# A gated FFT-mixer and token-MLP kernel: front, D-pass columns, inverse order and stores rearranged

## The chip, the cores and the metric

The kernel runs on one core of a Trainium2 chip (trn2). The metric is the device time of one execution in microseconds (us). The engines are TensorE (PE, with its weight loads PEld), VectorE (DVE), ScalarE (ACT), GpSimd (POOL) and SyncE (SP), whose queue issues most of the transfers. ACT and POOL can issue transfers too.

## The reference, cut to what matters

```python
def _A_ref(x, w_r, w_i):                # x: (1, 2048, 512) bf16
    X = rfft2(x.astype(float32))        # over tokens and channels
    return irfft2(X * (w_r + 1j * w_i), s=(2048, 512)).astype(bfloat16)

def _B_ref(x, w1, b1, w2, b2):          # w1: (2048, 1792), w2: (1792, 2048)
    h = _layernorm(x)                   # over the 512 channels, eps 1e-5
    u = gelu_tanh(einsum("bsd,sf->bdf", h, w1) + b1)
    return (einsum("bdf,fs->bds", u, w2) + b2).transpose(0, 2, 1)

x = A_x
g = sigmoid((x * gate_w).sum(-1, keepdims=True))
out = g * _A_ref(x, A_w_r, A_w_i) + (1 - g) * _B_ref(x, B_w1, B_b1, B_w2, B_b2)
```

All inputs are bf16. The tokens are cut into 16 blocks of 128.

## The kernel before, in words

Two computations share PE. The token MLP is the large one; the Fourier filter is cut into small matrix products between DVE butterflies.

**Front.** SP issues the loads of x (`load_x`, L90) and of the first 1024 columns of w1 (`load_w1a`, L93) in turn, in growing pieces; x blocks 4 and 5 come in one load. The two bias vectors go as rows into `brow` by two loads on ACT's queue (L120, L121). PE multiplies a zero tile, `warm`, ten times (L238), turns the biases into columns with one product against an identity (L240, `pb`), and starts the first MLP product (`mm1`, L271): for each of the first 12 blocks its 8 feature tiles, then, tile by tile in the order 0, 2, 4, 6, 1, 3, 5, 7, the last four blocks, each tile followed by its gelu on ACT (L336). The u tiles 0 to 5 lie in three PSUM pairs of two banks; tiles 0 and 1 share a pair.

**Layer norm.** For blocks 0 to 5 DVE does the statistics (`bstat`, L245), the aggregate (L249) and an addition of eps (L251), POOL raises to the power -0.5 (L254), and DVE normalises (`norm_dve`, L267). Blocks 6 to 15 go in pairs: aggregate on DVE, small operations on POOL (L251, L253, L254, L258), normalisation on ACT (`norm`, L263). Beside this ACT makes the sine tables: TD from DVE's angles (`angles_d`, `sines_d`), the angles for TA (L292, L293), TA (`sines_a`).

**Filling.** From the end of `mm1` (L271) on the program's order on PE is written by a small planner at build time. `products()` yields the remaining 128x512 products one by one: w1's other 6 tiles (L430), then w2's 15 blocks of 14 products (L439), each block ended by ACT's scale and bias (L442, `tbv`) and, late, by `final`. `fill(n)` takes n of them, `fill_to(t)` takes them until the planner's clock, which begins at 33.2 and gains 0.2165 a product, has reached t; `spent` adds the time of Fourier products. The constants T_TA, T_TB, T_IA, T_IB and T_Y say at which clock the token pass of YA, that of YB, the two inverses and the output scaling are put in.

**Fourier part.** DVE folds x into YA and YB (L365 to L419). For each of four residues r, `token` (L482, L485, L486) multiplies with the token tables into a PSUM pair, which ACT copies to ZA or ZB (L487); `dpass` (L494) multiplies with the channel tables TD into a pair, whose copy (L496) interleaves the two halves t of each column. DVE then splits, applies the filter and sums (`split`, `weights`, `sums`). `inverse` runs per residue `inv_tok` (L611, L617) and `inv_d` (L632), each emptied by ACT (`evac`, L589). There are three PSUM pairs in all, used in turn; a product into a pair waits until its last content is copied. DVE adds the residues up (L658 to L697), ACT and DVE scale with the gate, and DVE forms the filter's output `ap_` (L718 to L727).

**Gate.** DVE multiplies x with gate_w (`gprod`), ACT sums each block (`gacc`, L282, 16 blocks), then a tanh (L549) and three POOL operations give omg, gs and ombb2. ACT's w2 blocks need omg and ombb2.

**End.** `final(b)` adds ap_ to tbv on DVE (L730) and stores on SP (L731). The last block is done in two halves of 256 columns (L749), each ended by one DVE operation (L751) and its store (L753); ACT adds the bias to its part of ap_ before (L744). `hook` calls `final` for the blocks that the planner emits after T_Y + 12; those done by then are added in one loop.

Of the kernel before, what the change touches and what calls it, by code (L numbers as in the profile page):

```python
# [11 lines left out]
BF16 = mybir.dt.bfloat16  # L12
# [11 lines left out]
T_TA, T_TB, T_IA, T_IB, T_Y = 45.3, 56.8, 71.0, 83.8, 102.4  # L24
# [19 lines left out]
def kernel(  # L44
# [47 lines left out]
    def load_w1a(b0, b1):  # L92
        nc.sync.dma_start(out=w1a[b0 // 4][:, b0 % 4:(b1 - 1) % 4 + 1], in_=w1v[:, b0:b1, 0:FT1 * P])  # L93
# [24 lines left out]
    load_x(0, 1)  # L118
    brow = small.tile([NFT + NB, P], BF16, name="brow")
    nc.scalar.dma_start(out=brow[0:NFT], in_=B_b1.rearrange("(ft f) -> ft f", f=P))  # L120
    nc.scalar.dma_start(out=brow[NFT:NFT + NB], in_=B_b2.rearrange("(b a) -> b a", a=P))  # L121
    for b in range(3):
        load_x(b + 1, b + 2)
        load_w1a(b, b + 1)
# [16 lines left out]
    consts = small.tile([P, 5], F32, name="consts")  # L141
# [4 lines left out]
    nc.vector.memset(consts[:, 4:5], 1536.0)  # L146
    c_mpi, c_pi, c_mhalf = consts[:, 0:1], consts[:, 1:2], consts[:, 2:3]
# [86 lines left out]
    warm = small.tile([P, D], BF16, name="warm")  # L234
    nc.vector.memset(warm[:], 0.0)  # L235
# [188 lines left out]

    def products():
# [63 lines left out]
    def dpass(r, Z, cs):  # L489
        pr = pair("dp")  # L490
        for q, (sc, lst, t) in enumerate(((0, 0, 1), (1, 1, 0), (1, 2, 0), (0, 2, 1))):
            for c in range(2):
                o = 2 * c + q // 2
                nc.tensor.matmul(pr[:, sc, o * P:(o + 1) * P], lhsT=Z[:, r, q, c], rhs=TD[:, lst, t],  # L494
                                 start=True, stop=True)
        nc.scalar.copy(cs[:, :, r].rearrange("p x (j t) -> p x t j", t=2),  # L496
                       pr[:].rearrange("p h (c t j) -> p (h c) t j", c=2, t=2))
# [45 lines left out]
    for r in range(4):  # L543
# [3 lines left out]
    gacc(12, 16)  # L547
# [9 lines left out]
    fill_to(T_TB)  # L557
    ZB = H(6, [P, 4, 4, 2, P], "ZB")
    for r in range(4):
        token(1, r, ZB, YB)  # L560
        spent(0.87)
        fill(2)
# [25 lines left out]
    def evac(out, pr):  # L588
        nc.scalar.copy(out, pr[:].rearrange("p h n -> p (h n)"))  # L589
        act[0] = max(act[0], clock[0] + 0.1) + 1.01  # L590
# [31 lines left out]
    def inv_d(g, r, R, Hh):  # L622
        room()
# [10 lines left out]
        spent(0.44)  # L634
        evac(Hh[:, r].rearrange("p c n -> p (c n)"), pr)

    def inverse(g, UV, gslot, hslot, order):
# [97 lines left out]
    def hook(b):  # L735
        final(b)
# [44 lines left out]
```

## Time and profile before

| What | us |
|---|---|
| median of 3 runs (lowest, highest) | 130.16 (129.43, 131.82) |
| the profiled execution's own time | 130.46 |
| its span, from first to last instruction | 128.0 |
| ten zero products, first start to last end | 1.32 to 5.69 |
| first product of `mm1` starts | 5.74 |
| last x load for blocks 4 and 5 lands | 9.14 |
| ACT idle between the angle rows and its first normalisation | 8.48 to 14.91 |
| first product of w1's other tiles (L430) starts | 33.79 |
| token pass YA starts, YB starts | 45.87, 56.98 |
| inverse products begin, A and B | 71.77, 84.41 |
| DVE's first output addition (L730) | 116.42 |
| last PE product starts its group (L749) | 120.80 |
| last store issued | 125.09 |

The execution's own time is larger than the span, which runs from its first to its last instruction. A row of the groups gives line, engine, operation, output<-input, shape and count, then the busy time, the mean of one in ns, and the engine's idle time just before. A row of the timeline gives start, length, engine and line; what stands in square brackets is the idle time before it and what ended it. The chain of waits is read from top to bottom: start, length, what ran. Ends of PE products are modelled by the profiler, so the distance between starts tells more than a length. The granted PE clock is 1.00 in the whole span.

### The profile page before, as it was taken

The page shows a single profiled execution, that of the slowest core. Times are in us where ns is not written, and L with a number is a line of the kernel's source. Part 1 is how long each engine was busy: PE and PEld are TensorE (multiplying, and loading weights), DVE is VectorE, ACT ScalarE, POOL GpSimd, SP SyncE. Part 2 cuts the span into 40 slices and gives each one's busy share as a digit, 9 for nine tenths or more (in the row PEclk, how much of TensorE's full clock was granted, in tenths as well). Part 3 has the DMA queues.
Part 4 walks back from the last instruction along what each step waited for, and adds up shares of the span by engine and source line. Part 5 has one row for each costly group of instructions (what it writes and reads, how often), then busy time and mean ns, then how long its engine had stood idle before and what let it go on. Part 6 is the DMA issues. An engine that isn't in the chain of part 4 may idle for free.

```text
span 128.0 us, 2044 instructions
## 1 busy us (share of the span) xinstructions
PE 122.3 (96%) x737; PEld 65.4 (51%) x737; DVE 113.9 (89%) x197; ACT 89.9 (70%) x133; POOL 39.5 (31%) x69
## 2 busy tenths in 40 slices
PE   5999999999999999999999999999999999999970
PEld 2344444444444467657664676468544444444560
DVE  6969999999999999959999999999679999899840
ACT  4660359799999948999998499529975289922220
POOL 7633288999987429702100000000000000000000
PEclk9999999999999999999999999999999999999999
DMA  3899999998799999999994005400000000001872
GB/s 97 256 308 363 380 376 356 292 285 277 138 188 257 342 294 297 290 291 289 290 270 123 0 0 164 128 0 0 0 5 0 0 0 3 0 0 56 269 249 85
DMA packets 32906, 22.46 MB, mean 175 GB/s; under 512 B 5216, under 2 KB 30304, under 8 KB 32896
## 3 DMA queue, kind: packets, MB, share of 16 engines
q1 hardware_dynamic: 32484, 21.14, 59.7%
q0 software_dynamic: 352, 1.18, 2.9%
q8 instruction: 5, 0.08, 0.3%
q14 instruction: 5, 0.04, 0.1%
q10 hardware_dynamic: 60, 0.01, 0.0%
HBM read 19.15 MB, written 2.10 MB: 166 GB/s over the span
## 4 chain that ended last, share of the span: by engine, by line
PE 65%; ACT 11%; POOL 7%; DVE 5%; DMA 4%; SPq 2%; issue 2%
PE yb L439 35%; PE u L430 11%; PE ivt L617 5%; DMA xa<-in_A_x_dram 4%; POOL rstd L254 4%; ACT csA L496 3%; PE ivd L632 3%; PE u L271 3%; DVE stats L245 2%; PE yb L749 2%; ACT junk L282 2%; ACT gl L336 2%; PE tok L485 1%; PE dp L494 1%; PE tok L486 1%
## 5 line engine op out<-in xcount | busy, mean ns | idle before, releaser
L439 PE MATMUL yb<-gl,w2t 128*128 128x512 bf16 x210 | 47.5, 379 | 0.0
L439 PEld LDWEIGHTS <-w2t 128*128 128x128 bf16 x210 | 20.3, 98 | 22.2
L271 PE MATMUL u<-hn,w1a 128*128 128x512 bf16 x128 | 28.1, 379 | 0.1
L430 PE MATMUL u<-hn,w1b 128*128 128x512 bf16 x96 | 23.0, 379 | 0.0
L442 ACT ACTIVATE tbv<-yb,ombb,omg 128x512 bf16<-128x512 f32 x15 | 11.8, 789 | 14.3 <-PE yb L439 14.3
L271 PEld LDWEIGHTS <-w1a 128*128 128x128 bf16 x128 | 12.4, 97 | 15.4 <-issue 0.7
L430 PEld LDWEIGHTS <-w1b 128*128 128x128 bf16 x96 | 9.1, 98 | 8.4
L282 ACT ACTIVATE junk<-prod 128x512 bf16<-128x512 bf16 x16 | 10.1, 630 | 0.4
L589 ACT CAST R<-ivt 128x1024 bf16<-128x1024 f32 x8 | 8.1, 1037 | 3.0 <-PE ivt L617 3.0
L254 POOL TENSOR_TENSOR rstd<-mv,consts 128x1 f32<-128x1 f32 (+1 forms) x11 | 7.8, 708 | 6.6 <-DVE mv L251 6.5
L336 ACT ACTIVATE gl<-u,bcol 128x512 bf16<-128x512 f32 x14 | 9.0, 690 | 0.2 <-PE u L271 0.2
L589 ACT CAST H<-ivd 128x1024 bf16<-128x1024 f32 x8 | 8.3, 1062 | 0.0
L263 ACT ACTIVATE hn<-xb,nmr,rstd 128x512 bf16<-128x512 bf16 x8 | 6.1, 804 | 2.4 <-POOL nmr L258 2.4
L245 DVE BATCH_NORM_STATS2 stats<-xa 128x6 f32<-128x512 bf16 x8 | 5.5, 687 | 1.1 <-DMA xa<-in_A_x_dram 1.1
L263 ACT ACTIVATE hn<-xa,nmr,rstd 128x512 bf16<-128x512 bf16 x2 | 1.5, 806 | 6.4 <-DVE nmr L260 6.4
L730 DVE TENSOR_TENSOR tbv<-tbv,ap 128x512 bf16<-128x512 bf16 x15 | 5.2, 419 | 0.6 <-ACT tbv L442 0.6
L487 ACT CAST ZA<-tok 128x1024 bf16<-128x1024 f32 x4 | 4.0, 1012 | 2.4 <-PE tok L482 1.5
L238 PE MATMUL pw<-warm 128*128 128x512 bf16 x10 | 4.4, 624 | 1.3 <-DVE warm L235 1.3
L516 DVE TENSOR_TENSOR tatb<-PMA,wn 128x1024 bf16<-128x1024 bf16 x8 | 5.0, 690 | 0.2 <-issue 0.2
L245 DVE BATCH_NORM_STATS2 stats<-xb 128x6 f32<-128x512 bf16 x8 | 5.2, 676 | 0.0
L496 ACT CAST csB<-dp 128x1024 bf16<-128x1024 f32 x4 | 5.1, 1371 | 0.0
L516 DVE TENSOR_TENSOR tatb<-PMB,wn 128x2048 bf16<-128x2048 bf16 x4 | 4.7, 1227 | 0.2
(187 smaller groups left out, 221.0 us busy)
## 6 DMA issues: line engine op xcount, KB each, us to landing
w2t<-in_B_w_dram SPq DMA_DIRECT2D x8, 896.0 KB, 10.1
w1b<-in_B_w_dram SPq DMA_DIRECT2D x3, 1024.0 KB, 16.6
w1a<-in_B_w_dram SPq DMA_DIRECT2D x2, 1024.0 KB
out_dram<-tbv SPq DMA_DIRECT2D x15, 128.0 KB, 1.8
w1a<-in_B_w_dram SPq DMA_DIRECT2D x4, 256.0 KB, 3.2
w1a<-in_B_w_dram SPq DMA_DIRECT2D x2, 512.0 KB, 6.6
xb<-in_A_x_dram SPq DMA_DIRECT2D x2, 512.0 KB, 7.7
xa<-in_A_x_dram SPq DMA_DIRECT2D x4, 128.0 KB, 2.6
```

The source lines that it names most:

```text
L245: nc.vector.bn_stats(out=stats[:, b, :], in_=xh[b // 8][:, b % 8, :])
L254: nc.gpsimd.tensor_tensor(rstd[:, b0:b1], mv[:, b0:b1, 1], c_mhalf.to_broadcast([P, b1 - b0]), op=Alu.pow)
L263: nc.scalar.activation(hn[:, b, :], xh[b // 8][:, b % 8, :], ActF.Identity, bias=nmr[:, b:b + 1], scale=rstd[:, b:b + 1])
L271: nc.tensor.matmul(u1[ft], lhsT=w1a[b // 4][:, b % 4, ft * P:(ft + 1) * P], rhs=hn[:, b, :], start=(b == 0), stop=(b == NB - 1))
L282: nc.scalar.activation(junk[:], prod[b // 8][:, b % 8], ActF.Copy, accum_out=glog[:, b:b + 1])
L336: nc.scalar.activation(gl[:, ft, :], src, ActF.Gelu_apprx_tanh, bias=b1f[:, ft:ft + 1], scale=1.0)
L430: nc.tensor.matmul(u[:], lhsT=w1b[c][:, b, k * P:(k + 1) * P], rhs=hn[:, b, :], start=(b == 0), stop=(b == NB - 1))
L439: nc.tensor.matmul(y[:], lhsT=w2t[b // 2][:, ft, (b % 2) * P:(b % 2 + 1) * P], rhs=gl[:, ft, :], start=(ft == 0), stop=(ft == NFT - 1))
L442: nc.scalar.activation(tbv[0][:, b], y[:], ActF.Identity, bias=gate["ombb2"][:, b:b + 1], scale=gate["omg"][:, b:b + 1])
L496: nc.scalar.copy(cs[:, :, r].rearrange("p x (j t) -> p x t j", t=2), pr[:].rearrange("p h (c t j) -> p (h c) t j", c=2, t=2))
L516: mul(tt[:, i, :, r:r + n], PM[:, 2 * s:2 * s + 2, r:r + n], w[:, None].to_broadcast([P, 2, n, 256]))
L589: nc.scalar.copy(out, pr[:].rearrange("p h n -> p (h n)"))
```

## The change

The pieces, in the order of the program:

- The first block of w1 is loaded on ACT's queue, second after x block 0; the two bias loads move to SP, behind x block 1.
- `warm` is 128 columns wide instead of 512 and is zeroed first; eight zero products, each streaming it four times, instead of ten; the bias product stands ahead of the eighth.
- Blocks 0 and 1 get 1/sqrt(var + eps) from a square root on ACT and a reciprocal on DVE instead of an addition and POOL's power. ACT's first table is the one with the root; the sine's table and the sines come after block 1's root and the bias copy.
- The w2 blocks' ACT step goes through a list (`waiting`, `flush`), and is held back while the second inverse is emitted.
- `dpass` writes each product to every second PSUM column, so that the copy is straight.
- The accumulations `gacc` are spread: 4, 3, 3, then four singly after the D passes of A, two within the token pass of YB; the gate's operations follow that. The residues of YA go in the order 2, 0, 3, 1.
- The inverse's steps go t3, t1, d3, d1, t0, t2, d0, d2; the last residue 0 of B is copied out by DVE. The planner's time of a copy is 0.905 instead of 1.01.
- The last but one block's store goes on ACT's queue; the bias addition for the last block (L744) moves up behind block 13.
- The five T constants are earlier by 3.1, 1.4, 1.2, 1.2 and 2.6.

```diff
-T_TA, T_TB, T_IA, T_IB, T_Y = 45.3, 56.8, 71.0, 83.8, 102.4
+T_TA, T_TB, T_IA, T_IB, T_Y = 42.2, 55.4, 69.8, 82.6, 99.8
...
     def load_w1a(b0, b1):
-        nc.sync.dma_start(out=w1a[b0 // 4][:, b0 % 4:(b1 - 1) % 4 + 1], in_=w1v[:, b0:b1, 0:FT1 * P])
+        (nc.scalar if b0 == 0 else nc.sync).dma_start(out=w1a[b0 // 4][:, b0 % 4:(b1 - 1) % 4 + 1], in_=w1v[:, b0:b1, 0:FT1 * P])
...
     load_x(0, 1)
+    load_w1a(0, 1)
+    load_x(1, 2)
     brow = small.tile([NFT + NB, P], BF16, name="brow")
-    nc.scalar.dma_start(out=brow[0:NFT], in_=B_b1.rearrange("(ft f) -> ft f", f=P))
-    nc.scalar.dma_start(out=brow[NFT:NFT + NB], in_=B_b2.rearrange("(b a) -> b a", a=P))
-    for b in range(3):
+    nc.sync.dma_start(out=brow[0:NFT], in_=B_b1.rearrange("(ft f) -> ft f", f=P))
+    nc.sync.dma_start(out=brow[NFT:NFT + NB], in_=B_b2.rearrange("(b a) -> b a", a=P))
+    for b in range(1, 3):
         load_x(b + 1, b + 2)
         load_w1a(b, b + 1)
...
+    warm = small.tile([P, P], BF16, name="warm")
+    nc.vector.memset(warm[:], 0.0)
...
+    nc.vector.memset(consts[:, 5:6], 1e-5)
...
-    for _ in range(10):
-        nc.tensor.matmul(pw[:], lhsT=warm[:, 0:P], rhs=warm[:], start=True, stop=True)
     pb = bank("pb")
-    nc.tensor.matmul(pb[:, 0:NFT + NB], lhsT=brow[:], rhs=ident[:], start=True, stop=True)
+    for n in range(8):
+        if n == 7:
+            nc.tensor.matmul(pb[:, 0:NFT + NB], lhsT=brow[:], rhs=ident[:], start=True, stop=True)
+        nc.tensor.matmul(pw[:].rearrange("p (n k) -> p n k", n=4), lhsT=warm[:],
+                         rhs=warm[:, None, :].to_broadcast([P, 4, P]), start=True, stop=True)
...
-    nc.scalar.activation(sink[:], consts[:, 2:3], ActF.Sin, bias=c_mpi, scale=0.0)
+    nc.scalar.activation(sink[:], consts[:, 5:6], ActF.Sqrt, bias=consts[:, 5:6], scale=1.0)
     angles_d()
-    sines_d()
+
+    def root(b):
+        nc.vector.bn_aggr(out=mv[:, b, :], in_=stats[:, b, :])
+        nc.scalar.activation(rstd[:, b:b + 1], mv[:, b, 1:2], ActF.Sqrt, bias=consts[:, 5:6], scale=1.0)
+
+    for b in range(2):
+        bstat(b)
+        root(b)
+        if b == 1:
+            bstat(2)
+        nc.vector.reciprocal(rstd[:, b:b + 1], rstd[:, b:b + 1])
+        norm_dve(b)
...
     nc.scalar.copy(bcol[:], pb[:, 0:NFT + NB])
+    nc.scalar.activation(sink[:], consts[:, 2:3], ActF.Sin, bias=c_mpi, scale=0.0)
+    sines_d()
...
-    bstat(0)
-    aggr(0, 1)
-    for b in range(NDVE):
+    aggr(2, 3)
+    for b in range(2, NDVE):
...
+    waiting, hold = [], [False]
+
+    def flush(keep=0):
+        while len(waiting) > keep:
+            b, y = waiting.pop(0)
+            nc.scalar.activation(tbv[0][:, b], y[:], ActF.Identity, bias=gate["ombb2"][:, b:b + 1],
+                                 scale=gate["omg"][:, b:b + 1])
+            hook(b)
+            act[0] = max(act[0], clock[0] + 0.3) + 0.7
...
         for b in range(NB - 1):
+            flush(1)
...
-                    nc.scalar.activation(tbv[0][:, b], y[:], ActF.Identity, bias=gate["ombb2"][:, b:b + 1],
-                                         scale=gate["omg"][:, b:b + 1])
-                    hook(b)
-                    act[0] = max(act[0], clock[0] + 0.3) + 0.7
+                    waiting.append((b, y))
+                    if not hold[0]:
+                        flush()
...
-                o = 2 * c + q // 2
-                nc.tensor.matmul(pr[:, sc, o * P:(o + 1) * P], lhsT=Z[:, r, q, c], rhs=TD[:, lst, t],
-                                 start=True, stop=True)
-        nc.scalar.copy(cs[:, :, r].rearrange("p x (j t) -> p x t j", t=2),
-                       pr[:].rearrange("p h (c t j) -> p (h c) t j", c=2, t=2))
+                o = pr[:, sc].rearrange("p (c j t) -> p c j t", c=2, t=2)[:, c, :, q // 2]
+                nc.tensor.matmul(o, lhsT=Z[:, r, q, c], rhs=TD[:, lst, t], start=True, stop=True)
+        nc.scalar.copy(cs[:, :, r], pr[:].rearrange("p h (c m) -> p (h c) m", c=2))
...
-    for q in range(3):
-        gacc(4 * q, 4 * q + 4)
-        fill(16)
+    gacc(0, 4)
+    fill(16)
+    gacc(4, 7)
+    fill(16)
+    gacc(7, 10)
     fill_to(T_TA)
     ZA = H(8, [P, 4, 4, 2, P], "ZA")
-    for r in range(4):
+    for r in (2, 0, 3, 1):
         token(0, r, ZA, YA)
...
-    for r in range(4):
+    for r in (2, 0, 3, 1):
         dpass(r, ZA, csA)
...
-    gacc(12, 16)
+    for b in range(10, 14):
+        gacc(b, b + 1)
+        fill(4)
+    fill_to(T_TB)
+    ZB = H(6, [P, 4, 4, 2, P], "ZB")
+    for r in range(4):
+        token(1, r, ZB, YB)
+        spent(0.87)
+        if r % 2:
+            gacc(14 + r // 2, 15 + r // 2)
+        fill(2)
...
-        act[0] = max(act[0], clock[0] + 0.1) + 1.01
+        act[0] = max(act[0], clock[0] + 0.2) + 0.905
...
-    def inv_d(g, r, R, Hh):
-        room()
+    def inv_d(g, r, R, Hh, late=False):
+        if not late:
+            room()
...
+        if late:
+            return pr
         evac(Hh[:, r].rearrange("p c n -> p (c n)"), pr)
...
-        landed = []
-        for i in range(5):
-            if i < 4:
-                inv_tok(g, order[i], UV, R)
-                landed.append(act[0])
-            if i > 0:
-                fill_to(landed[i - 1] + 0.1)
-                inv_d(g, order[i - 1], R, Hh)
-        return Hh
+        landed, kept = {}, None
+        for step, r in (("t", 3), ("t", 1), ("d", 3), ("d", 1), ("t", 0), ("t", 2), ("d", 0), ("d", 2)):
+            if step == "t":
+                inv_tok(g, r, UV, R)
+                landed[r] = act[0]
+            else:
+                fill_to(landed[r] + 0.1)
+                kept = inv_d(g, r, R, Hh, late=(g == 1 and r == 0)) or kept
+        return Hh, kept
...
     fill_to(T_IB)
-    HB = inverse(1, PMB, 6, 1, (3, 1, 0, 2))
-    fill_to(T_IB + 10.6)
+    hold[0] = True
+    HB, prB = inverse(1, PMB, 6, 1)
+    hold[0] = False
+    flush()
+    fill_to(T_IB + 10.2)
...
     sub(sv[:, 2:4], HB[:, 3], HB[:, 1])
+    nc.vector.tensor_copy(HB[:, 0].rearrange("p c n -> p (c n)"), prB[:].rearrange("p h n -> p (h n)"))
...
-        nc.sync.dma_start(out=out2[b * P:(b + 1) * P, :], in_=tbv[0][:, b])
+        (nc.scalar if b == NB - 2 else nc.sync).dma_start(out=out2[b * P:(b + 1) * P, :], in_=tbv[0][:, b])
...
+    apl = ap_[1][:, NB - 9]
+
     def hook(b):
+        if b == NB - 3:
+            nc.scalar.activation(apl, apl, ActF.Identity, bias=ombb2[:, NB - 1:NB], scale=1.0)
         final(b)
...
-    apl = ap_[1][:, b - 8]
-    nc.scalar.activation(apl, apl, ActF.Identity, bias=ombb2[:, b:b + 1], scale=1.0)
```

More of the change, by code (lines that the diff above doesn't have):

```diff
@@ L139 @@
     load_w(1)
-    consts = small.tile([P, 5], F32, name="consts")
+    warm = small.tile([P, P], BF16, name="warm")
+    nc.vector.memset(warm[:], 0.0)
+    consts = small.tile([P, 6], F32, name="consts")
     nc.vector.memset(consts[:, 0:1], -PI_IN)
@@ L232 @@
     prod = [WS(6, [P, 8, D], "prod0"), WS(7, [P, 8, D], "prod1")]
-    warm = small.tile([P, D], BF16, name="warm")
-    nc.vector.memset(warm[:], 0.0)
     pw = bank("pw")
-    for _ in range(10):
-        nc.tensor.matmul(pw[:], lhsT=warm[:, 0:P], rhs=warm[:], start=True, stop=True)
     pb = bank("pb")
-    nc.tensor.matmul(pb[:, 0:NFT + NB], lhsT=brow[:], rhs=ident[:], start=True, stop=True)
+    for n in range(8):
[3 more added lines that the diff above has]
+                         rhs=warm[:, None, :].to_broadcast([P, 4, P]), start=True, stop=True)
     pu = [pair(f"u1_{i}") for i in range(3)]
@@ L556 @@
     gate["omg"], gate["ombb2"] = omg, ombb2
[L557 to L562, printed above, removed]
     csB = H(4, [P, 4, 4, 256], "csB")
@@ L634, in inv_d, with inverse @@
         spent(0.44)
+        if late:
+            return pr
         evac(Hh[:, r].rearrange("p c n -> p (c n)"), pr)
-    def inverse(g, UV, gslot, hslot, order):
+    def inverse(g, UV, gslot, hslot):
         R = H(gslot, [P, 4, 2, 4, P], f"R{g}")
         Hh = H(hslot, [P, 4, 2, D], f"H{g}")
-        landed = []
-        for i in range(5):
-            if i < 4:
-                inv_tok(g, order[i], UV, R)
-                landed.append(act[0])
-            if i > 0:
-                fill_to(landed[i - 1] + 0.1)
-                inv_d(g, order[i - 1], R, Hh)
-        return Hh
+        landed, kept = {}, None
[7 more added lines that the diff above has]
+        return Hh, kept
     fill_to(T_IA)
-    HA = inverse(0, PMA, 7, 8, (3, 1, 0, 2))
+    HA, _ = inverse(0, PMA, 7, 8)
     fill_to(T_IB)
-    HB = inverse(1, PMB, 6, 1, (3, 1, 0, 2))
-    fill_to(T_IB + 10.6)
+    hold[0] = True
[3 more added lines that the diff above has]
+    fill_to(T_IB + 10.2)
     EO = big.tile([P, 16, D], BF16, tag="wt", name="EO")
```

## The prediction

> **What bounds the kernel now.** I read the page's busy shares first, then the chain of work that ended last, then the timeline at the places where the chain leaves TensorE (PE), and last the SyncE queue's own timeline at the end.
>
> ```profile
> span 128.0 us, 2044 instructions
> PE 122.3 (96%) x737; PEld 65.4 (51%) x737; DVE 113.9 (89%) x197; ACT 89.9 (70%) x133; POOL 39.5 (31%) x69
> ```
>
> PE is busy 96% of the span, so time is won only where PE starts, pauses, or ends. The chain:
>
> ```profile
> 4.02 5.12 DMA xa<-in_A_x_dram
> ...
> 25.73 1.52 ACT hn L263 x2
> 27.25 1.04 ACT TA L192
> 28.29 0.02 issue
> 28.30 1.28 ACT L336
> 29.59 0.01 issue
> 29.60 0.69 ACT gl L336
> 30.29 0.04 issue
> 30.34 3.61 PE u L271 x16
> 33.95 12.09 PE u L430 x56
> ```
>
> Until 30.34 PE is not what is late. The load of x blocks 4 and 5 lands at 9.14; from there statistics and normalisation run on VectorE (DVE), POOL and ScalarE (ACT) without a gap to block 15 (25.73 to 27.25); then come a sine table, a table load, the first gelu, and only then the second half of the first product's last blocks. PE itself ran from 5.74: 112 products by 0.2158 us (56 of L439 take 12.25 us with a last one of 0.38) would end at 29.90. So 0.44 us of PE's early start is lost by 30.34. After that PE is nearly gapless: to 124.03 there is one visible pause, a token product that waits for a PSUM pair that ACT empties late.
>
> ```profile
> 61.35 0.27 PE L485 MATMUL tok<-TA,YB 128*128 128x256 bf16 x1 [0.28 <-ACT ZB L487]
> ```
>
> The two products before it began at 60.47 and last 2 x 0.216, so PE was free at 60.91: 0.44 us. DVE has two waits, both for ACT's emptying of PSUM:
>
> ```profile
> 56.77 1.23 DVE L501 TENSOR_TENSOR PMA<-csA 128x2048 bf16<-128x2048 bf16 x1 [1.52 <-ACT csA L496]
> 93.65 0.43 DVE L676 TENSOR_TENSOR sv<-H 128x512 bf16<-128x512 bf16 x1 [1.98 <-ACT H L589]
> ```
>
> At the end the last result is ready at 124.54, but its store is issued at 125.09: SP is still working off the stores that DVE released in a burst from 116.42.
>
> ```profile
> 124.06 0.48 DVE L751 SCALAR_TENSOR_TENSOR tbv<-yb,omg,ap 128x256 bf16<-128x256 f32 x1 [0.96 <-PE yb L749]
> ```
> ```profile
> 122.79 1.74 SPq L731 DMA_DIRECT2D out_dram<-tbv  x3
> 124.62 0.38 SPq L753 DMA_DIRECT2D out_dram<-tbv  x1
> 125.09 0.40 SPq L753 DMA_DIRECT2D out_dram<-tbv  x1
> ```
>
> **The change part by part.**
>
> *Front, blocks 0 and 1.* From the start of the aggregate (3.69) to the start of the normalisation (4.76) the trace has 1.07 us: aggregate 0.18, DVE add 0.15, POOL power 0.58, hand-overs. The new path is aggregate, a root on ACT (nearest row: the 128x1 activations, 0.28), a DVE reciprocal (nearest: 128x1 tensor_scalar, 0.15): about 0.75, so block 0 is ready near 4.85 instead of 5.17. Eight zero products at 0.427 instead of ten, begun 0.35 earlier by the smaller, earlier memset, free PE by about 4.4. But the bias product, ahead of the eighth, now waits for bias loads that are third and fourth on SP (issued about 1.7 to 2.5; early loads land 2.2 to 3.2 us after issue), so 4.3 to 5.3, and all real products queue behind it. PE starts between 4.9 and 5.9. I give this nothing either way: what PE gains before 30.34 it waits there, and it may start as late as 5.74 + 0.44 = 6.18 without harm. Block 1 is about 0.25 later than before (statistics of block 2 are put ahead of its reciprocal), ready at 6.8, needed at 6.6 at the earliest; same cover.
>
> *The load of x 4 and 5.* SP loses the first weights (0.43) and gains two bias issues (0.65 and 0.33 on ACT's queue), so blocks 2 and up are issued up to 0.6 later. The first weights go out at 0.72 on ACT's queue, ahead of the table load. DMA share is 0.74 to 0.98 from 2.0 to 5.0 us, so the bytes rather than the issues mostly set landing, and the same bytes start sooner. DVE waits 0.88 for this load, so a shift passes 1:1 to 30.34: bounds -0.44 (then PE's own start binds again) and +0.6. I take 0.
>
> *ACT's front.* The root before the sines brings one more table load; bias copy, sines (3 x 0.6), the two angle rows (2.4) and the scalar one (0.3) come after root 1 at about 6.0 and end near 12.4. The next ACT work starts at 14.91 after 6.4 us idle, so 2.5 us of cover remain: cost 0. The Trainium skill (ScalarE: Activation LUTs, What ACT_TABLE_LOAD costs) charges a set switch 1.28 us for the load and 1.38 us for a drain, which speaks against this edit; the rows show 1283 ns and the neighbouring instructions 0.01 to 0.02 us away, no drain. By the page ACT's front would end near 13.8, still covered.
>
> *Middle: column order, moved accumulations, token order.* The D passes now write their products to every second PSUM column, and ACT copies straight. The straight copies of the same size (L487) take 1.01 against 1.33 to 1.37: ACT saves 0.3 x 8. With T_TA 3.1 earlier, the token pass of YA starts at about 43.0 (planner clock plus 0.75, as at 33.95 against 33.2); its first operands are complete at 41.2, the last at 44.5, needed at 46.4. csA then ends near 53 instead of 56.73, before DVE finishes YB (55.25): the 1.52 wait goes. The YB token pass starts near 55.9, 0.6 after YB is complete. The last accumulations (4 x 0.75) no longer stand ahead of ZB's copies, so PE's 0.44 us at 61.35 goes. The gate is about 3 us later (62.7), as is the w2 load behind it on SP (about 10 us to land, its products after 90): covered.
>
> *Does a step of two columns slow PE?* This trace has no such product. Nearest from one side: products written in runs of 64 (L482) against whole rows (L494):
>
> ```profile
> L494 PE MATMUL dp<-TD,ZA 128*128 128x128 bf16 x32 | 2.4, 220 | 0.0
> L482 PE MATMUL tok<-TA,YA 128*128 128x128 bf16 x8 | 0.6, 219 | 0.0
> ```
>
> Broken runs cost nothing there. From the other side, the slowest pace for one shape here is twofold (zero products 0.427 against 0.216): a pass of eight then takes 0.90 instead of 0.45, 8 x 0.45 = +3.6, all on PE. A gain is excluded, since 128, 256 and 512 columns take 0.056, 0.109 and 0.216: columns set the time, not their places. I take 0, the L482 row being nearest, with less trust than elsewhere. The Trainium skill (PSUM — Partial Sum Buffer, Specifications) says that PSUM has 8-byte lines and any non-contiguous pattern slows matmuls significantly. L482 contradicts "any"; a step of two leaves half of each line unused, which no run here shows. By the page the sum would lie on the slower side, by the row on the faster.
>
> *Inverse.* Two token steps, then two D steps, output copies held back, and the last block emptied by DVE (L751 takes 0.48 for 256 columns from PSUM; four times the columns about 1.3). DVE: -1.52 - 1.98 + 1.3 = -2.2, so the final additions start near 114.2. T_IA and T_IB move 1.2 forward, DVE's operands 1.5, so PE meets no new wait; each margin is about 0.5. PE does the same products: 0.
>
> *End.* Stores start 2.2 us sooner, and one goes out on ACT's queue. Thirteen at 0.475 end near 121, before the first half of the last block (123.1). The last store is then issued about 0.05 after its data: -0.5. ACT's bias addition (0.71) moves into a 2.2 us idle gap: 0.
>
> Sum: -0.44 - 0.5 = -0.94 on a span of 128.0, so 127.06. The profiled execution took 130.46 (2.46 around the span): 129.52. The median of the runs, 130.16, is 0.30 under that execution, so I predict 129.2.
>
> **The rivals.**
>
> 1. *Stepped PSUM writes slow the D passes (slower than before).* For it: PE has no slack after 30.34. Against it: L482. Place: L494's successor. It outweighs the gains from 0.12 us a pass, 15 ns a product; at twofold 129.2 + 3.6 = 132.8.
> 2. *The front becomes later.* Either x 4 and 5 land 0.6 later (129.8), or PE's pause before the bias product keeps its slow pace: before, the full pace came only after 4.4 us of zero products. Ten real products at half pace from 5.2 lose 10 x 0.211 = 2.1 against a cover of 0.98: +1.1, 130.3. It decides from five such products.
> 3. *The front pays.* The load lands 0.44 or more earlier and PE's start counts up to 0.84 as well: 128.0 to 128.8, say 128.3.
>
> **How the numbers follow.** Forecast 0.45 (own range 128.6 to 129.8, for margins of half a microsecond and the spread of runs), stepped writes 0.33 (130.8 to 132.8 by their factor), later front 0.15, front pays 0.07. The range 128.2 to 132.8 leaves out little more than the tails. 2%, about what a measurement of this kernel can tell from no change, is 127.56 and 132.76. Faster than that: 0.04, the edge of rival 3. Slower: 0.14, the upper part of rival 1. The rest, 0.82, is within.
>
> **What would show it.** The D passes: eight products in 0.45 us or in up to 0.9. The restart after the first gelu near 30.3 whatever PE's start. No ACT wait at the YB tokens; L501 without its 1.52. SP idle before the last store, issued within 0.1 of its data. Wrong if the D pass lengthens, if statistics of block 4 begin after 9.5, or if early real products follow at 0.43.

## The result and the profile after

The changed kernel takes 133.83 us (median of 6 runs, 133.58 to 134.56) where the kernel before takes 129.8 in the same comparison (6 runs, 129.34 to 131.82). The ratio is 1.0311, 95% interval 1.0245 to 1.0377: slower. (Here and below a ratio leaves disturbed runs out and a median takes all runs, so the two differ a little.) The prediction was 129.2, with a range up to 132.8 and "slower" at 0.14. It was wrong in direction and in size.

The profiled execution took 134.0, of which 132.2 is the span. The page's first lines are the span and each engine's busy time:

```profile
span 132.2 us, 2030 instructions
PE 126.1 (95%) x723; PEld 68.7 (52%) x735; DVE 114.9 (87%) x199; ACT 89.6 (68%) x136; POOL 39.9 (30%) x67
```

PE's share is 95% where it was 96%, but of a longer span: PE is busy 3.8 us longer, although it has two zero products less to do. The chain of waits (start, length, what ran) shows where:

```profile
2.14 3.00 DMA brow<-in_B_b_dram
5.14 0.14 issue
5.27 0.18 PE pb L243
5.45 0.54 PE pw L244
5.99 10.88 PE u L276 x41
16.93 10.74 PE u L276 x49
27.72 7.93 PE u L276 x36
35.65 2.81 PE u L457 x13
...
49.51 0.87 PE dp L521 x8
```

Two things are to be seen. The chain no longer runs through x blocks 4 and 5 and the first gelu: it comes from the bias load and then stays on PE, which ends the first product at 35.65 instead of 33.95, 1.70 later. And eight products of the D pass take 0.87 us instead of 0.45, in each of the eight passes. The groups of PE (count, then busy time and mean ns of one) set the stepped writes beside the runs of 64 that the prediction relied on:

```profile
L521 PE MATMUL dp<-TD,ZA 128*128 128x128 bf16 x32 | 4.1, 309 | 0.0
L509 PE MATMUL tok<-TA,YA 128*128 128x128 bf16 x8 | 0.6, 219 | 0.0
```

One stepped product lasts 309 ns by the record and follows the last by 0.87 / 8 = 0.109 us; a product of the same shape in runs of 64 stays at 219 and 0.056. The front's timeline (start, length; in brackets the idle time before and what ended it) shows the other loss. First the statistics of blocks 0 and 4 in the kernel before, then the changed kernel:

```profile
2.96 0.69 DVE L245 BATCH_NORM_STATS2 stats<-xa 128x6 f32<-128x512 bf16 x1
9.17 0.69 DVE L245 BATCH_NORM_STATS2 stats<-xa 128x6 f32<-128x512 bf16 x1 [0.88 <-DMA xa<-in_A_x_dram]
```
```profile
0.97 3.17 PE L244 MATMUL pw<-warm 128*128 128x512 bf16 x7 [0.97 <-DVE warm L144]
3.55 0.69 DVE L250 BATCH_NORM_STATS2 stats<-xa 128x6 f32<-128x512 bf16 x1 [0.50 <-DMA xa<-in_A_x_dram]
5.27 0.18 PE L243 MATMUL pb<-ident,brow 30*128 30x30 bf16 x1 [1.14 <-DMA brow<-in_B_b_dram]
5.79 0.15 PEld L276 LDWEIGHTS <-w1a 128*128 128x128 bf16 x1 [0.28 <-issue]
6.21 0.15 PEld L276 LDWEIGHTS <-w1a 128*128 128x128 bf16 x1 [0.28 <-issue]
10.46 0.69 DVE L250 BATCH_NORM_STATS2 stats<-xa 128x6 f32<-128x512 bf16 x1 [1.45 <-DMA xa<-in_A_x_dram]
```

The zero products are done at 4.14, PE stands still for 1.14 until the biases land, and the weights of the real products then follow each other at 0.43 us, half pace, ten times, up to 10.02. Block 0's statistics begin at 3.55 (before 2.96), block 4's at 10.46 (before 9.17), each after a wait for its load. What the DMA engines did meanwhile is in the windows of the transfers. Columns: stretch, length, granted PE clock, DMA share, GB/s. First the kernel before, then the changed one:

```profile
3.50:4.00 0.50, 1.00 0.98 340
4.00:4.50 0.50, 1.00 0.93 279
4.50:5.00 0.50, 1.00 0.84 303
```
```profile
3.50:4.00 0.50, 1.00 0.41 104
4.00:4.50 0.50, 1.00 0.70 166
4.50:5.00 0.50, 1.00 0.56 162
```

SP issues one load in about 0.43. Two of its early places now go to bias rows of a few KB, and for a while the DMA engines move less: 104 to 166 GB/s instead of 279 to 340. That this is what made the load of x 4 and 5 late is likely, but argued from the order of the issues. Block 0's load has another neighbour: the first weights (256 KB) now leave on ACT's queue at 0.72, together with it, where they left at 1.66.

The gains that the prediction counted are there. PE no longer waits for ACT at a YB token product, and at the end the last stores leave as soon as DVE is done:

```profile
127.08 0.36 ACTq L769 DMA_DIRECT2D out_dram<-tbv  x1
127.85 1.86 SPq L793 DMA_DIRECT2D out_dram<-tbv  x2
128.87 0.48 DVE L791 SCALAR_TENSOR_TENSOR tbv<-yb,omg,ap 128x256 bf16<-128x256 f32 x1 [1.04 <-PE yb L789]
```

The last result is ready at 129.35, against 124.54 before: +4.81. Of this 8 x 0.42 = 3.36 is the D passes, 1.70 the first product, -0.44 the token wait that is gone; 0.19 is left over. From the last result to the end it is 2.85 instead of 3.46, which gives the 4.2 of the two spans.

### The profile page after: what moved, and what is told of

It is laid out like the page before. It is cut to its first block, busy times and chain, and to the rows that moved or that the text cites. A ratio compares the mean times of both kernels' runs of the same rounds, so it can differ in the third digit from the quotient of the medians.

```text
span 132.2 us, 2030 instructions
## 1 busy us (share of the span) xinstructions
PE 126.1 (95%) x723; PEld 68.7 (52%) x735; DVE 114.9 (87%) x199; ACT 89.6 (68%) x136; POOL 39.9 (30%) x67
## 4 chain that ended last, share of the span: by engine, by line
PE 93%; DMA 2%; SPq 1%; issue 1%; DVE 0%
PE yb L467 34%; PE u L276 22%; PE u L457 16%; PE dp L521 5%; PE ivt L648 5%; PE ivd L664 3%; PE tok L512 2%; PE yb L789 2%; PE tok L513 2%; DMA brow<-in_B_b_dram 2%; SPq L90 1%; PE ivt L642 0%; PE pw L244 0%; DVE tbv L791 0%; SPq L122 0%
## 5 line engine op out<-in xcount | busy, mean ns | idle before, releaser
L467 PE MATMUL yb<-gl,w2t 128*128 128x512 bf16 x204 | 46.4, 379 | 0.3
L276 PE MATMUL u<-hn,w1a 128*128 128x512 bf16 x126 | 29.8, 399 | 0.1
L276 PEld LDWEIGHTS <-w1a 128*128 128x128 bf16 x128 | 13.1, 102 | 16.7 <-issue 3.0
L457 PEld LDWEIGHTS <-w1b 128*128 128x128 bf16 x96 | 9.7, 104 | 7.9
L259 POOL TENSOR_TENSOR rstd<-mv,consts 128x2 f32<-128x2 f32 (+1 forms) x9 | 6.7, 744 | 9.0 <-DVE mv L256 9.0
L620 ACT CAST H<-ivd 128x1024 bf16<-128x1024 f32 x7 | 7.0, 1045 | 0.8 <-PE ivd L664 0.8
L522 ACT CAST csA<-dp 128x1024 bf16<-128x1024 f32 x4 | 4.0, 1012 | 1.6 <-PE dp L521 1.5
L664 PEld LDWEIGHTS <-R 128*128 128x128 bf16 x64 | 3.8, 98 | 2.5 <-ACT R L620 2.5
L664 PE MATMUL ivd<-TI,R 128*128 128x128 bf16 x64 | 4.9, 220 | 0.0
L244 PE MATMUL pw<-warm 128*128 128x512 bf16 x8 | 3.8, 627 | 1.0 <-DVE warm L144 1.0
```

The source lines that it names most:

```text
L259: nc.gpsimd.tensor_tensor(rstd[:, b0:b1], mv[:, b0:b1, 1], c_mhalf.to_broadcast([P, b1 - b0]), op=Alu.pow)
L276: nc.tensor.matmul(u1[ft], lhsT=w1a[b // 4][:, b % 4, ft * P:(ft + 1) * P], rhs=hn[:, b, :], start=(b == 0), stop=(b == NB - 1))
L457: nc.tensor.matmul(u[:], lhsT=w1b[c][:, b, k * P:(k + 1) * P], rhs=hn[:, b, :], start=(b == 0), stop=(b == NB - 1))
L664: nc.tensor.matmul(pr[:, c, o * P:(o + 1) * P], lhsT=plane(par, cos), rhs=TI[:, lst, t], start=True, stop=True)
```

## The experiments

The theory after the two traces: two losses that add up, (a) the stepped PSUM writes, 3.4 us, and (b) the later front. The rivals: the D pass is slow for another reason, such as its operands or ACT's copies; the front's part is only the pace after PE's pause; or only the late loads. Times are medians in us; the ratio is to the kernel before in the same comparison. "Straight" is the D pass of before in the changed kernel.

| kernel | us | before | ratio (95%) |
|---|---|---|---|
| e1, straight | 129.66 | 130.08 | 0.9969 (0.9925, 1.0014) |
| e2, kernel before with the stepped D pass | 133.13 | 130.08 | 1.0235 (1.0194, 1.0276) |
| e3, changed with the front of before | 132.35 | 130.08 | 1.0172 (1.0129, 1.0216) |
| e4, straight, front of before | 128.86 | 130.08 | 0.9918 (0.9873, 0.9962) |
| e5, straight, loads of before | 129.04 | 130.19 | 0.9915 (0.9879, 0.9951) |
| e6, straight, 12 zero products | 129.36 | 130.19 | 0.9965 (0.9931, 0.9999) |
| e8, D pass in runs of two columns | 130.80 | 130.19 | 1.0051 (1.0018, 1.0085) |
| e10, e4 with x ahead of weights | 128.87 | 130.19 | 0.9923 (0.9888, 0.9958) |
| e11, changed kernel again | 133.35 | 130.13 | 1.0217 (1.0156, 1.0277) |
| e12, changed with the loads of before | 132.80 | 130.13 | 1.0186 (1.0125, 1.0248) |
| e13, straight, front on two queues | 128.93 | 130.13 | 0.9862 (0.9797, 0.9928) |
| e14, e1 again | 130.88 | 130.13 | 1.0021 (0.9977, 1.0065) |
| e15, e1 a third time | 130.37 | 129.90 | 1.0053 (1.0021, 1.0084) |
| e16, e6 again | 129.30 | 129.90 | 0.9946 (0.9915, 0.9976) |
| e17, changed with 12 zero products | 132.70 | 129.90 | 1.0241 (1.0181, 1.0301) |
| e18, runs of two, front of e13 | 128.64 | 129.90 | 0.9901 (0.9862, 0.9940) |

### Each loss alone: e1 to e4

e1 puts the straight D pass back, e2 puts the stepped one alone into the kernel before:

```diff
-                o = pr[:, sc].rearrange("p (c j t) -> p c j t", c=2, t=2)[:, c, :, q // 2]
-                nc.tensor.matmul(o, lhsT=Z[:, r, q, c], rhs=TD[:, lst, t], start=True, stop=True)
-        nc.scalar.copy(cs[:, :, r], pr[:].rearrange("p h (c m) -> p (h c) m", c=2))
+                o = 2 * c + q // 2
+                nc.tensor.matmul(pr[:, sc, o * P:(o + 1) * P], lhsT=Z[:, r, q, c], rhs=TD[:, lst, t],
+                                 start=True, stop=True)
+        nc.scalar.copy(cs[:, :, r].rearrange("p x (j t) -> p x t j", t=2),
+                       pr[:].rearrange("p h (c t j) -> p (h c) t j", c=2, t=2))
```

> The changed kernel with the D passes of before (products to whole PSUM columns, ScalarE interleaves). Theory (stepped writes and a late front add up): the pass falls from 0.87 to 0.45 us, eight of them, so 133.8 - 3.4 = 130.4. Rival (the products were only hiding another wait, ScalarE's slower copies or the DVE chain): 131.5 or more, with new idle time on TensorE. Rival 2 (the front is the whole loss): 133.5.

> The kernel before with nothing but the stepped D passes and their straight copy. Theory: + 8 x 0.42, less up to 0.44 for the token wait that ScalarE's shorter copies may remove: 129.8 + 2.9 to 3.4 = 132.7 to 133.2. Rival (the slow pass is a matter of the new order around it, not of the addresses): 129.4 to 130.

e3 keeps the stepped pass and takes back the front (loads, zero products, roots); e4 takes back both. The heart of that edit:

```diff
-    load_w1a(0, 1)
-    load_x(1, 2)
...
-    nc.sync.dma_start(out=brow[0:NFT], in_=B_b1.rearrange("(ft f) -> ft f", f=P))
+    nc.scalar.dma_start(out=brow[0:NFT], in_=B_b1.rearrange("(ft f) -> ft f", f=P))
...
-    for b in range(2):
-        bstat(b)
-        root(b)
...
+    aggr(0, 1)
```

> The changed kernel with the front of before: loads, ten zero products, power on GpSimd for blocks 0 and 1; stepped writes stay. Theory: the first product ends near 33.9 instead of 35.6, so 133.8 - 1.7 = 132.1. Rival (TensorE only waits later for DVE): 133.5.

> The changed kernel with the front and the straight D passes of before: what is left is order, inverse, stores. Theory: the gains of the prediction are real, 129.8 - 0.9 = 128.9, with no ScalarE wait at the YB tokens and the last store issued within 0.1 us of its data. Rival: they are not, 129.8 or above.

The stepped pass costs 133.13 - 130.08 = 3.05 in the kernel before and 132.35 - 128.86 = 3.49 in the changed one with the old front: the term (a), about 8 x 0.42. In e2 it is the only edit, and ACT's copy, which goes with it, became shorter (1.01 instead of 1.33 to 1.37), so no other cause is left. Its passes last as in the changed kernel:

```profile
50.55 0.87 PE dp L494 x8
51.42 0.65 PE u L430 x3
52.07 0.87 PE dp L494 x8
```

The front costs 129.66 - 128.86 = 0.8 with the straight pass and, against the changed kernel's 133.83 from the first comparison, 1.5 with the stepped one. e1 came 0.7 below the 130.4 expected of it; the repeats below bear on that. Everything that is neither front nor D pass wins: e4 is at 0.9918, about 1.1 us faster than before.

### How many columns make a run: e8 and e18

e8 writes runs of two neighbouring fp32 columns (8 bytes) instead of single ones, and ACT's copy sorts them:

```diff
-                o = pr[:, sc].rearrange("p (c j t) -> p c j t", c=2, t=2)[:, c, :, q // 2]
+                o = pr[:, sc].rearrange("p (c j t u) -> p c j t u", c=2, t=2, u=2)[:, c, :, q // 2]
...
+        nc.scalar.copy(cs[:, :, r].rearrange("p x (j u t) -> p x j t u", u=2, t=2),
+                       pr[:].rearrange("p h (c j t u) -> p (h c) j t u", c=2, t=2, u=2))
```

> The changed kernel with products written in runs of two columns (8 bytes) with a gap of two, instead of every second column; ScalarE's copy puts them in order, so the result is the same. Theory (half of an 8-byte line per column is what costs): the pass takes 0.45 us again and the time is 129.7. Rival (any broken pattern as short as this costs): 0.87 us and 133.8.

e8's groups of the D pass and of w1's other tiles:

```profile
L521 PE MATMUL dp<-TD,ZA 128*128 128x128 bf16 x32 | 2.4, 219 | 0.0
...
L457 PE MATMUL u<-hn,w1b 128*128 128x512 bf16 x96 | 23.5, 379 | 1.8 <-DMA w1b<-in_B_w_dram 1.8
```

The pass is back at 219 ns and 0.45 for eight, so it is not the broken pattern as such that costs, but runs of a single column, which use half of each pair. (Runs of two that begin at an odd column were not run.) The total, 130.80, was not the 129.7 hoped for. In the profiled execution, at 131.92 the longest of the ten, SP's issue of a transposing load (L347) lasted 9.22 us, where it took 3.74 in the changed kernel; the last load of w1b behind it left late, and PE waited 1.8 for it. That might have been a price of the runs of two, so e18 tried them with a front that is not late:

> The D pass in runs of two columns (8 bytes), copied out in that order, with the front of the two-queue kernel (biases, then the first weights, on ACT's queue; x 4 and 5 ahead of the third weights; ten zero products; roots on POOL). Theory 'whole 8-byte lines are free': D passes at 0.45 us (219 ns), total 128.9 as with the straight pass, a little less if ACT's shorter copies (1.02 for 1.33) free a pair earlier anywhere. Rival 'runs of two columns have a price that the first such run showed' (130.8 with the changed front): 130.1 or more here, even where no load is late.

e18 took 128.64, ratio 0.9901; in its profiled execution (130.33, the longest of its ten) the transposing load took 3.60 and the passes 0.45. Runs of two columns cost nothing that is seen here. e8's 130.80 is also within the range of the straight kernel with the same front (129.66, 130.37, 130.88). Why the transposing load sometimes takes twice as long to issue (7.39 in e10, too, where nothing waited for it) stays open.

### The front: loads or pace

e5 gives the straight kernel the loads of before, with eight zero products and ACT's roots kept. e6 keeps the new loads and makes twelve zero products, so that PE does not stop:

```diff
-    for n in range(8):
-        if n == 7:
+    for n in range(12):
+        if n == 11:
```

> The straight-column version of the changed kernel with the loads of before (first weights on SyncE, biases on ScalarE's queue); eight zero products and ScalarE's roots stay. Theory (the two bias issues on SyncE starve the transfers and hold up the bias product): x 4 and 5 land near 9.2 to 9.8 and the time falls from 129.7 to that of the whole front undone, 128.9. Rival (the eight zero products or the roots cost it): it stays at 129.7.

> The straight-column version of the changed kernel with twelve zero products instead of eight, so that TensorE does not pause before the bias product. Theory (the late load stands right behind the slow pace): the products that ran at 0.43 us are gone or fewer, but the restart after the first gelu stays near 30.9, so 129.4 to 129.7 against 129.7. Rival (the slow pace alone is the front's loss): 128.9.

e5 is as fast as e4 (0.9915 and 0.9918): zero products and roots cost nothing that is seen; the loads do. (With the loads of before the biases also land in time, so e5 has no pause before the bias product.) e6 has its first product at full pace from 5.70 and its restart after the gelu at 30.47, where e5 has 30.08. The rival "pace alone" falls: its 128.9 would be a ratio of 0.990, below e6's interval. So the new loads cost about 0.3 to 0.4 by themselves (0.39 in the restart, 0.32 between the medians, whose intervals just overlap). The other profiles agree: the restart is at 30.47 to 30.85 in all seven with the new loads and full pace, and at 30.03 to 30.40 in five of the six with the loads of before in their old order; the sixth, e4's, has 30.94, after a wait of 1.61 for x 4 and 5.

Which load is late is not what the first profile suggests. In e11, the changed kernel again, DVE waits for x block 0 and then for no load up to block 4:

```profile
4.06 0.69 DVE L250 BATCH_NORM_STATS2 stats<-xa 128x6 f32<-128x512 bf16 x1 [1.01 <-DMA xa<-in_A_x_dram]
9.44 0.69 DVE L250 BATCH_NORM_STATS2 stats<-xa 128x6 f32<-128x512 bf16 x1
```

So it is in all nine profiles in which the first weights leave on ACT's queue at 0.72: block 0's statistics begin at 3.55 to 4.13, after a wait of 0.50 to 1.09 for its load. In the nine others they begin at 2.96 or 2.97 without a wait, also in e13 and e18, where the first weights leave on that queue at 1.75, behind the biases. Block 4 begins at 9.14 to 9.52 without a wait in eight of the nine; only the first profile waits for x 4 and 5, to 10.46. The dip of the transfers near 3.5 to 4.0 is in all nine too (79 to 172 GB/s, against 289 to 383 in the others), but in eight DVE waits for no load behind it. The first weights beside block 0 are thus the likelier cause of most of the front's late loads; no run moves them alone. Of the 0.6 to 1.2 only a part reaches the restart, since with the loads of before DVE waits later, for x 4 and 5 (0.33 to 1.61). e10 asks whether x 4 and 5 could be brought still earlier in e4, with x ahead of the second and third weights (the lines show the edit against the changed kernel):

```diff
-    for b in range(1, 3):
-        load_x(b + 1, b + 2)
-        load_w1a(b, b + 1)
+    load_x(2, 3)
+    load_x(3, 4)
+    load_w1a(1, 2)
...
+    load_w1a(2, 3)
```

> The version with both undone (128.9), with the loads of x 3 and of x 4 and 5 put ahead of the second and third weights. Theory: DVE no longer waits for x 4 and 5 (0.9 to 1.6 us), the restart after the first gelu is set by TensorE's own start, so 0.3 to 0.6 less: 128.4. Rival (weights come too late instead, or the pace at the start decides): 128.9 or more.

Block 4's statistics began at 8.26, 0.9 earlier than in the kernel before, and PE then ran all 128 products without a stop, but they ended at 33.72, and the time stayed that of e4 (0.9923), not the 128.4 of the theory. There PE's own start had become the bound, as the prediction said of an early front. Next, the changed kernel and e1 were repeated, and e12 took the loads of before into the changed kernel alone:

```diff
-        (nc.scalar if b0 == 0 else nc.sync).dma_start(out=w1a[b0 // 4][:, b0 % 4:(b1 - 1) % 4 + 1], in_=w1v[:, b0:b1, 0:FT1 * P])
+        nc.sync.dma_start(out=w1a[b0 // 4][:, b0 % 4:(b1 - 1) % 4 + 1], in_=w1v[:, b0:b1, 0:FT1 * P])
...
-    load_w1a(0, 1)
-    load_x(1, 2)
...
+    nc.scalar.dma_start(out=brow[0:NFT], in_=B_b1.rearrange("(ft f) -> ft f", f=P))
```

> The changed kernel once more, on the same chip and beside the straight-column version, because stepped writes cost 4.2 us there against 3.5 and 3.1 in the two other pairs. Theory (the terms add up: stepped 3.4, front 0.6, against 0.9 of gains): 130.1 + 3.1 = 133.2, and 3.4 above the straight version. Rival (late front and stepped writes make each other worse): 134 or more, 4.2 above the straight version.

> The changed kernel with the loads of before and nothing else undone (stepped writes stay). Theory (in the front only the loads cost): 0.6 below the changed kernel of this call, 132.5, as with the whole front undone (132.35). Rival (roots or zero products have a share that shows only beside the stepped writes): 133 or more.

> The straight-column version of the changed kernel once more, beside the changed kernel on one chip. Theory: 129.7 (0.5 under the kernel before), 3.4 under the changed kernel of this call. Rival: 4.2 under it.

e11 gave 133.35 and e12 132.80, about as expected. e14 missed: 130.88 where e1 had 129.66 with the same code. The weight loads of the first products tell the two profiles apart; in e14 they come one by one, as in the changed kernel's first profile,

```profile
6.23 0.15 PEld L276 LDWEIGHTS <-w1a 128*128 128x128 bf16 x1 [0.27 <-issue]
6.66 0.15 PEld L276 LDWEIGHTS <-w1a 128*128 128x128 bf16 x1 [0.28 <-issue]
```

0.43 apart until 9.62, with the first product's end at 35.46. In e1 eight of them fit into 1.60 us from 6.07 on, and the end is at 34.46. So after the pause the pace differs from one execution to the next, and with it 1.0 us. The length of the pause does not decide it: half pace followed 1.14 and 0.62, full pace 0.55 to 1.38 (e15, e11, e8, e1). In this comparison the stepped pass costs only 133.35 - 130.88 = 2.47, not the 3.4 expected; that fits an e11 at full pace and an e14 at half, as profiled. Whether the pause is to blame was the last question: e15 (with it) and e16 (twelve zero products, without), beside each other, and e17, the changed kernel with twelve:

> The changed kernel with the straight D pass of before, eight zero products (the pause before the bias product stays). Theory 'the pace varies': TensorE's products after the pause run at full or at half pace from one execution to the next, so the spans of the runs fall into two groups, near 127.4 (first weights about 0.21 apart, end of the first product at 34.4) and near 128.5 (0.43 apart until about 9.6, end at 35.5), some us apart whatever the chip; the median lies between 129.6 and 130.9. Rival 'chip or day': the two earlier results (129.66 and 130.88) come from something else, and the spans lie in one group.

> The same with twelve zero products, so that TensorE does not stop before the bias product. Theory 'the pace varies': with the pause gone the slow group goes, all spans within 127.0 to 127.7, median 129.4 on the same chip and in the same minutes as the kernel with the pause. Rival 'chip or day': spans and median move with those of the kernel with the pause, whatever they are.

> The changed kernel as it is, with twelve zero products instead of eight and nothing else. Theory 'loads and stepped writes decide, the pause adds when the pace is half': the D passes stay at 0.87 us (309 ns by product), the restart is at 30.5 to 30.8, and the median is 129.4 + 3.4 = 132.8, in spans of one group near 130.6. Rival 'the pause costs nothing': 133.4 to 133.8, as the changed kernel measured.

With the pause the spans of 12 runs lie between 127.5 and 129.1, most of them at 128.1 or more; without it ten of 12 lie at 127.4 or 127.5. The medians differ by 1.07, the ratios' intervals do not touch. Four more zero products, which close the pause, save time, then. It is not their number alone: e5 has eight, stops for no more than 0.42 before its first product, starts it at full pace, and none of its ten spans is above 127.4. That the pause costs by the half pace is shown for two executions (the first profile of the changed kernel, and e14) and only argued for the rest; the two separate groups of spans that e15's theory foresaw are not seen. Nor does half pace need a pause: in e4, with ten zero products and none, the weights follow each other at 0.43 from 6.26 to 7.11, in e13 from 5.88 to 6.31. e15's own profile is one of the spans above 128 for another reason: its products run at full pace from 5.78, and its span is 128.3 because 3.85 us pass from the last result to the end, where e16 has 2.88. That late last store is not explained. The stepped pass, too, stands clear here. e17's chain, then e16's:

```profile
30.49 3.61 PE u L276 x16
34.10 9.06 PE u L457 x42
47.96 0.87 PE dp L521 x8
```
```profile
30.62 3.61 PE u L276 x16
34.24 9.06 PE u L457 x42
48.09 0.45 PE dp L521 x8
```

The fronts are equal within 0.14, the passes are not, and the medians differ by 132.70 - 129.30 = 3.40, against 8 x 0.42 = 3.36.

### A version that beats both: e13

e13 is straight, with roots on POOL as before; the biases, then the first weights, go out on ACT's queue, x 4 and 5 ahead of the third weights, and ten zero products follow the early, small memset. The added loads alone:

```diff
+    nc.scalar.dma_start(out=brow[0:NFT], in_=B_b1.rearrange("(ft f) -> ft f", f=P))
+    nc.scalar.dma_start(out=brow[NFT:NFT + NB], in_=B_b2.rearrange("(b a) -> b a", a=P))
     load_w1a(0, 1)
...
+    load_x(2, 3)
+    load_w1a(1, 2)
+    load_x(3, 4)
     load_x(4, 6)
+    load_w1a(2, 3)
```

> Straight columns, power on GpSimd as before, biases and then the first weights on ScalarE's queue, SyncE's queue without them and with x 4 and 5 ahead of the third weights; zero tile set first, ten zero products. Theory (feed the transfers from two queues without putting small loads ahead of large ones): x 4 and 5 land near 8.3, TensorE starts near 5.4 and is not held at the first gelu, 128.3 to 128.6. Rival (x block 0 shares the engines with the first weights and comes later): 129 or more.

128.93, ratio 0.9862: the lowest ratio, though the median misses the 128.3 to 128.6 of the theory. PE starts at 5.46, is not held at the first gelu and ends the first product at 33.86; its first products run at half pace until 6.71. Against e4 (0.9918) the intervals overlap, so what its front adds is not settled; that it beats the kernel before is.

## Why the prediction was wrong

**What bounds the kernel.** Right: PE is the bound. The 0.42 that each D pass grew by went into the end in full (e17 against e16: 3.40 for 3.36).

**The stepped write.** This step failed: "I take 0, the L482 row being nearest, with less trust than elsewhere." L482 was near in the wrong respect. It breaks the row into runs of 64, which still fill both halves of every pair of columns; a step of two fills one half. The row could not speak for a half-filled pair, and the upper bound, twofold, was the value: +3.4 measured, +3.6 priced in rival 1. The page that the prediction weighed and set aside, the Trainium skill (PSUM — Partial Sum Buffer, Specifications), has 8-byte lines, and e8 agrees: runs of 8 bytes cost nothing, single 4-byte columns double the time. Its words "any non-contiguous" stay contradicted, by runs of 64 and of two.

**The front, blocks 0 and 1, and the load of x 4 and 5.** Also wrong, by less, and in two steps. The first: the root's path was timed rightly (aggregate at 4.28 to normalisation at 5.02, 0.74 for the forecast 0.75), but it was hung on a block 0 that comes as before, "so block 0 is ready near 4.85". The prediction has the first weights go out at 0.72 on ACT's queue and puts their effect on x block 0 at nothing; its statistics began 0.6 to 1.2 later in all nine profiles. "I take 0" for the load of x 4 and 5 held in eight of them (9.14 to 9.52, at most 0.35 after the kernel before); only in the first was it 1.29 late, outside the bound of 0.6. The second: PE's start was as bounded (5.78, between 4.9 and 5.9), but "I give this nothing either way" left the half pace to a rival. In the first profile it came as rival 2 has it: ten products at half pace lose 2.1, of which a start at 5.78 leaves 6.18 - 5.78 = 0.40 covered, so 1.7, as measured; the rival's +1.1 had a start at 5.2. The late load then lay hidden behind it: the first gelu began at 30.89 and lasts 0.69, so PE could have gone on near 31.6, but it came to its last 16 products only at 35.65 - 3.61 = 32.04. Of the two losses of the front the larger one counts; they do not add up.

A rule of the Trainium skill (TensorE: Matmul & The Clock Gate, Part 1) fits the pace: full speed comes after a busy window of some 3.4 us that runs free of the program. Here 3.17 us of zero products and a pause came before the half pace, 4.37 without a pause before the full pace of the kernel before. No run here shows the window itself: the granted clock reads 1.00 in both, also where the products go at half pace.

**ACT's front, middle, inverse.** Right, cost 0 as far as is seen: e5 keeps the roots and the zero products, and is as fast as e4. ACT's straight copies take 1.01, as expected, PE's wait at the YB tokens is gone, and so is DVE's 1.52 for csA. DVE's wait of 1.98 in the inverse did not go, it is 3.1 now; that costs nothing, since the stores of all whole blocks on SP are issued by 126.13, before the last block's first result at 127.82.

**End.** Right: the last store follows its result at once, and 2.85 remains instead of 3.46, 0.6 for the forecast 0.5. With the token wait the prediction summed -0.94; e4, which has these gains and neither loss, is 0.82% of 130 = 1.07 faster (0.5 to 1.65).

**The rivals.** All three signs of being wrong that the prediction named came in the first profile: the longer D pass, block 4's statistics after 9.5, real products at 0.43. The rivals were priced as if one excluded the other. Rival 1 (+3.6) and rival 2's pace (+1.1) have separate causes, one in the D pass, one at the start, and both came. Their own prices, added to the forecast, give 129.2 + 3.6 + 1.1 = 133.9; 133.83 was measured. That they agree so closely is luck: the stepped pass cost 3.36, the front 1.70, the execution took 1.8 more than its span and not 2.46, and the same kernel took 133.35 the next time. The range stopped at the first of them, and "slower" at 0.14 followed from that.

**What stays open.** The changed kernel gave 133.83 and 133.35 on two occasions; the pace after the pause could explain a difference of that size, but only one execution of each was profiled, and e11's ran at full pace. What sets the pace in the other executions, how the front's loss divides between the first weights and the biases, and why e15's last store is late, no run shows.

## What to carry to other kernels

Take the nearest row by the property that the edit changes, here how much of an 8-byte pair of fp32 columns each run fills, not by shape or line; if it is not in the trace, the bound that speaks against the change deserves the larger share, above all on an engine without slack. Let the copy do the interleaving, or write aligned runs of two or more fp32 columns. A load that is moved to a second queue still shares the DMA engines with the first: ask which transfer it now runs beside, and who waits for that one. One profile shows one execution: the late load of x 4 and 5 was in the first and in none of the eight others with these loads. Rivals with separate causes add up: the range must reach to their sum, not to the dearest of them.

## What the runs showed of the hardware that was not expected

- A TensorE product of 128 columns takes 0.109 us instead of 0.056 when it writes every second fp32 column of PSUM, and 0.056 again in runs of two or 64 columns.
- After 3.2 us of zero products and a pause of 0.6 to 1.4 us, the real products ran at half pace (0.43 us) for about 4 us in two profiled executions and at full pace in others of the same code, with a granted clock of 1.00 in both.
- With 256 KB of weights issued on ACT's queue at the same moment as x block 0 (128 KB) on SP's, DVE had to wait for block 0: its statistics began at 3.55 to 4.13 us in nine profiles, against 2.96 or 2.97 in the nine where the weights left about 1 us later.
- With two loads of a few KB in SP's early places (0.32 and 0.45 us of issue), the transfers fell to 79 to 172 GB/s between 3.5 and 4.0 us, against 289 to 383 without; in eight of nine profiles DVE waited for no load behind it.
- The issue of a transposing load on SP took 3.6 to 3.8 us in most profiles, 7.39 and 9.22 in two.
